# Forgetting attention and SwiGLU on one core: two query/key blocks turned by DMA, four wider gates, norm weights loaded in rows, an early table load and an order drawn from a list of seeds

## The chip, the cores and the metric

The kernel runs on one core of a Trainium2 chip. A core has TensorE (PE in the profile, with its weight loads shown apart as PEld), VectorE (DVE), ScalarE (ACT), GpSimd (POOL) and SyncE (SP), and 16 DMA engines that all of its queues share. The metric is the device time of one execution in microseconds (us); lower is better. The kernel before takes 385.1 us, the median of three runs (385.1, 385.17 and 381.8 us).

## The reference

```python
scores = scale * q @ k.T                            # 8 batches, 8 heads, 576 tokens, head size 64
cum = cumsum(log(clip(f, 1e-4, 1)))                 # a forget gate for each token and head
scores = where(causal, -1e9, scores + cum[i] - cum[j])
attn = softmax(scores);  o = attn @ v               # per batch and head
x = o, heads side by side                           # 4608 tokens x 512
xn = x / sqrt(mean(x * x) + 1e-6) * rms_g
g = xn @ w_gate;  val = xn @ w_val                  # 512 -> 1536
out = (g * sigmoid(g) * val) @ w_out                # 1536 -> 512
```

Inputs and output are f32.

## The kernel before

**The work.** A batch has 576 tokens: four blocks of 128 and one of 64 (the `LAST`). The decay needs no term in the scores: the `j` part, `exp(mid - cum[j])`, scales the rows of v (`scale_v`), an extra column of v carries the same factor so that the denominator comes out of the same matmul, and the `i` part cancels. So a block of attention is a score matmul (`score_block`, L444), an exp on ACT (L462), a causal mask on POOL for the diagonal block (L469), the values matmul (`values`, L488) and a division on DVE (L502, L504). `norm` then takes the squares on ACT (L520), the root on POOL (L524, L525), scales on ACT (L532) and turns the block, by PE and a DVE copy (L540, L548, L550) for batches 0 and 1 and by a DMA transpose on SP's queue (L554) for the others.

The feed-forward part works on nine groups of 512 tokens: groups 0 to 7 are the four whole blocks of batches 0 to 7, group 8 collects the eight 64-token rests. `gate` makes 512 columns of gate and of value: 4 matmuls of 128x512 each (one of the 12 slices of the inner width for all 512 tokens), or, in groups 0 and 1, 16 matmuls of 128x128 each (four slices for one block of 128 tokens, so that a gate waits for one block only). Then come tanh on ACT (L611) and two DVE operations (L613, L606). `project` multiplies with `w_out` (L624, three parts of 4 matmuls), ACT copies the result (L637) and SP stores it (L641, L650).

**How q and k are turned.** Scores need q and k with the head dimension in partitions. For batches 2 to 7 and for the 64-token rests of all batches, `turn` has SP issue one DMA transpose for q and one for k per block (L375). For the whole blocks of batches 0 and 1, `turn_pe` has PE transpose them and DVE (q) and ACT (k) copy them out of PSUM (L403): blocks 0 and 3 of batch 0 by themselves (L390), blocks 1 and 2 of batch 0, 0 and 1 of batch 1, and 2 and 3 of batch 1 in pairs (L396). A pair comes in by one load for q and one for k (`load_qk2`, L308: two rows of a head in one piece), a single block by `load_qk` (L296).

**The norm weights.** `rms_g` is loaded as 128 partitions x 4 by a DMA on ACT's queue behind the decay's exp (L268). Group 0's blocks are multiplied with it when they are copied (L548). For the others it is multiplied into `w_gate` and `w_val` by `weigh` (L338), after group 0 has used the plain weights.

**The decay.** One chain at the start: load f (SP), clip (DVE), ln (ACT, L255), cumulative sum (DVE, L261), exp (ACT, L266), five PE transposes (L275), copy (L279).

**What sets the order.** Nothing is written in order by hand. Each piece of work is a `Unit` with an engine, an assumed duration, a key, what it depends on, and the buffers it takes and gives back. `Plan.run` plays these through once on the host: whenever an engine is free it takes, of the units that are ready and whose buffers are free, the one with the smallest key. The order that results is the order of instructions on each engine, and each engine runs its own in order. DMA loads are played as an issue on the queue's engine (SP, ACT or POOL), a transfer that shares bandwidth with the other kind of queue (software for POOL, hardware for SP and ACT), and a landing time. Before the play, all keys are moved by a random amount of at most 0.02 (seed 12, L84 to L86).

Of the kernel before, what the change touches and what calls it, by code (L numbers as in the profile page):

```python
# [10 lines left out]
F32 = mybir.dt.float32  # L11
# [3 lines left out]
PSUM = bass.MemoryType.PSUM  # L15

# [16 lines left out]
class Plan:  # L33
# [8 lines left out]
    def add(self, eng, dur, key, emit, deps=(), take=(), give=(), lat=0.06):  # L42
# [32 lines left out]
    def run(self):  # L75
# [67 lines left out]
def fox_ffn_kernel(ctx, tc, q, k, v, f, moe_w_gate, moe_w_val, moe_w_out, moe_rms_g, out):  # L143
    nc = tc.nc
# [41 lines left out]
    rgT = sb.tile([128, NDC], F32, name="rgT")  # L186
    mhalf = sb.tile([128, NB], F32, name="mhalf")
# [13 lines left out]
    def pe(dur, key, emit, deps=(), take=(), give=()):  # L201
        return P.add("PE", dur, key, emit, deps, take, give, lat=0.22)

    def act(dur, key, emit, deps=(), take=(), give=()):
        return P.add("ACT", dur, key, emit, deps, take, give)

    def dve(dur, key, emit, deps=(), take=(), give=()):
        return P.add("DVE", dur, key, emit, deps, take, give)
# [3 lines left out]

    issues = {}

    def load(eng, issue, moves, key, emit, deps=(), take=(), give=(), late=1.6):
# [3 lines left out]
        u = P.add(eng, issue, key, emit, deps, list(take) + [lane], (), lat=2.0 if eng == "POOL" else 1.2)  # L219
# [5 lines left out]

    PLAIN = 1

# [29 lines left out]
    def emit_cum():  # L257
# [6 lines left out]

    d3 = dve(2.5, -19, emit_cum, [d2])
    d4 = act(0.9, -19, lambda: nc.scalar.activation(dec[:, 0:S], cum, ACT.Exp, scale=-1.0, bias=mid[:, 0:1]),  # L266
             [d3])
# [3 lines left out]
    h_dec = Hold("ff", 1 + EARLY)  # L271

    def emit_dect():
        for j in range(NB):
            nc.tensor.transpose(T_ff[h_dec.slot][:, j * 64:(j + 1) * 64], dec[:, j * 128:(j + 1) * 128],  # L275
                                ident_f[0:BH, 0:BH])

    d5 = pe(0.6, -19, emit_dect, [d4, iden_f], take=[h_dec])
# [11 lines left out]
    def load_qk(b, j, key):  # L290
        p0, n = rows(j)
        for src, nm in ((q, "q"), (k, "k")):
# [5 lines left out]
            qkload[b, nm, j] = load("POOL", 0.9 * n / 128, (8 * n, 0.0009), key, emit, take=[h])  # L298
            late.setdefault((b, j), []).append(issues[id(emit)])

    def load_qk2(b, j, key):

        t0 = j * 128
        for src, nm in ((q, "q"), (k, "k")):
# [5 lines left out]
            qkload[b, nm, j] = load("POOL", 0.9, (1024, 0.0016), key, emit, take=[h])  # L310

    def load_v(b, j, key):
# [7 lines left out]
        vload[b, j] = load(eng, dur, (64, 0.0155) if eng == "POOL" else (8 * n, 0.00117), key, emit, take=[h])  # L320
# [4 lines left out]
    def load_w(i, key):  # L325
        c0, c1 = i * 512, (i + 1) * 512
        for w, src, nm in ((wg, moe_w_gate, "g"), (wv, moe_w_val, "v")):
            def emit(w=w, src=src):
                nc.gpsimd.dma_start(out=w[:, :, c0:c1], in_=src[:, c0:c1].rearrange("(c p) f -> p c f", p=128))
            Lw[nm, i] = [load("POOL", 0.75, (512, 0.0061), key, emit, late=2.6)]  # L330
# [10 lines left out]
    def load_wo(key):  # L341
        for i in range(2):
# [4 lines left out]
            Lo.append(load("POOL", 0.85, (768, 0.0061), key, emit))  # L347
# [23 lines left out]
    def turn(b, j, key):  # L371
        p0, n = rows(j)
        for dst, nm in ((T_QT, "q"), (T_KT, "k")):
            def emit(dst=dst, nm=nm):
                nc.sync.dma_start_transpose(out=dst[hold_QT[b].slot][:, :, p0:p0 + n],  # L375
                                            in_=T_qk[hold_qk[b, nm, j].slot][0:n, :])
            turned[b, nm, j] = load("SP", 1.6, (4 * n, 0.00117), key, emit, [qkload[b, nm, j]],
                                    take=[hold_QT[b]], give=[hold_qk[b, nm, j]])
# [32 lines left out]
    def scale_v(b, j, key):  # L411
# [9 lines left out]
        add, dur, eng = (dve, 0.8 if b or j < EARLY else 1.2, nc.vector) if b < 2 else (pool, 1.3, nc.gpsimd)  # L421
# [89 lines left out]
    def norm(b, js, key):  # L511
# [4 lines left out]
        for i, j in enumerate(js):  # L516
# [4 lines left out]
            us.append(act(0.85, key, emit, [evac[b, j, 0], evac[b, j, 1]]))  # L521
# [5 lines left out]
        for i, j in enumerate(js):  # L527
# [6 lines left out]
            if g < 2:  # L534
# [9 lines left out]
                def cp(hf=hf, g=g, c=c):  # L544
                    tp = T_ff[hf.slot].bitcast(BF16)[:, 0:512].rearrange("p (c t) -> p c t", t=128)
                    to = T_of[g][hold_xT[g].slot][:, :, c:c + 128]
                    if g < PLAIN:
# [3 lines left out]
                pieces[b, j] = dve(0.69 if g < PLAIN else 0.42, key - 0.02, cp, [t, L_rg], take=[hold_xT[g]], give=[hf])  # L551
            else:
# [3 lines left out]
                pieces[b, j] = load("SP", 1.6, (4 * n, 0.00117), key, tr, [u], take=[hold_xT[g]], give=[hn])  # L556
# [12 lines left out]
    for b, qi in order:  # L569
        if b >= 2 or qi == LAST:  # L570
# [19 lines left out]
    def gate(g, key, deps, i, pairs):  # L590
# [22 lines left out]
        a = dve(0.72, key - 0.1, lambda: nc.vector.scalar_tensor_tensor(  # L613
            T_ga[ha.slot], in0=T_th[ht.slot], scalar=1.0, in1=T_ff[hg.slot], op0=ALU.add, op1=ALU.mult),
            [th], take=[ha], give=[ht, hg])
        return dve(0.72, key - 0.1, last, [a, uv], take=[hold_hT[g]], give=[ha, hv])

    def project(g, j, key):
        hf, ho = Hold("ff", 1), Hold("ores", 1)
        last = None  # L620
        for part in range(3):
# [5 lines left out]
            deps += hdone[g, j][part::3] if g < 2 else hdone[g, j][part * 4:part * 4 + 4]  # L627
# [25 lines left out]
    for g in range(G):  # L653
        if g < 2:
# [62 lines left out]
```

## Time and profile before

| | |
|---|---|
| runs | 385.1, 385.17, 381.8 us |
| the profiled execution, its own time | 382.67 us |
| its span | 380.9 us |
| PE, DVE, ACT, POOL busy | 94%, 57%, 62%, 53% |
| PE's clock as granted, mean | 0.997 |

A line of the profile names an engine, the line of the kernel, the operation and what it writes and reads. "Idle before" is the time in which the engine stood still just before such an instruction, and the name behind the arrow is what ended it. The times of several matmuls of a group overlap, because they are pipelined: sixteen 128x128 matmuls of 0.22 us each take 0.89 us together. "SPq" and "POOLq" are the queues that issue DMAs.

### The profile page before, as it was taken

Reading aid. Unit: us, or ns where it says so; the run is one execution under the profiler, and the core shown is the slowest. Engines: PE = TensorE matmul, PEld = TensorE weight load, DVE = VectorE, ACT = ScalarE, POOL = GpSimd, SP = SyncE. Lnnn points to the kernel's source line nnn. Section 1 sums busy time; section 2 is a strip of 40 time slices with the busy share of each in tenths; the row PEclk is TensorE's granted clock in tenths of the full one; section 3 lists DMA queues with packets and bytes.
Section 4 is the critical chain, followed back from the end, with each engine's and each line's share of the span. In section 5 each row is a group of like instructions: output and inputs, shape, how many; then the busy total and the mean of one; then the engine's idle time right before and its main releaser. Section 6 shows DMA issues by size and latency. Waiting matters only on the chain.

```text
span 380.9 us, 9695 instructions
## 1 busy us (share of the span) xinstructions
PE 358.7 (94%) x3941; PEld 212.4 (56%) x3941; DVE 218.0 (57%) x457; ACT 236.6 (62%) x377; POOL 200.6 (53%) x280
## 2 busy tenths in 40 slices
PE   1589799999999999999999999999999999999994
PEld 1479697788865455545555554455455544444441
DVE  4557998855555656544745565546655545454430
ACT  4486798778767676866676768665975433331321
POOL 8786579999799664964497369921411000000000
PEclk9999999999999999999999999999999999999998
DMA  9999999999999949995699979972120210100004
GB/s 147 180 202 220 214 98 174 142 190 170 164 187 179 163 95 147 142 167 80 98 183 147 106 108 165 199 65 56 36 58 28 57 34 29 55 28 29 28 29 110
DMA packets 129389, 44.84 MB, mean 118 GB/s; under 512 B 117824, under 2 KB 122432, under 8 KB 129344
## 3 DMA queue, kind: packets, MB, share of 16 engines
q0 software_dynamic: 76368, 23.34, 61.5%
q1 hardware_dynamic: 52368, 20.74, 29.2%
q8 instruction: 31, 0.51, 0.6%
q10 hardware_dynamic: 608, 0.13, 0.4%
q14 instruction: 14, 0.11, 0.1%
HBM read 37.90 MB, written 9.44 MB: 124 GB/s over the span
## 4 chain that ended last, share of the span: by engine, by line
PE 84%; DMA 5%; POOL 3%; ACT 3%; DVE 2%; issue 1%; SPq 0%; ACTq 0%; DVEq 0%; POOLq 0%
PE ff L599 45%; PE ff L624 24%; PE ff L488 7%; PE sc L444 6%; DMA qk<-in_k_dram 3%; DMA KT<-qk 2%; ACT PT L462 1%; POOL PT L469 1%; POOL qk L296 1%; ACT junk L520 1%; DVE x L504 1%; POOL v L319 1%; ACT th L611 0%; DVE xT L548 0%; DVE QT L403 0%
## 5 line engine op out<-in xcount | busy, mean ns | idle before, releaser
L613 DVE SCALAR_TENSOR_TENSOR ga<-th,ff 128x512 f32<-128x512 f32 x108 | 73.8, 685 | 85.4 <-ACT th L611 84.0
L624 PE MATMUL ff<-wo,hT 128*128 128x512 bf16 x432 | 108.9, 379 | 0.0
L611 ACT ACTIVATE th<-ff 128x512 f32<-128x512 f32 x108 | 64.3, 595 | 69.2 <-PE ff L599 59.8
L462 ACT ACTIVATE PT<-sc 128x1024 bf16<-128x1024 f32 x96 | 94.6, 1020 | 13.3 <-PE sc L444 13.1
L599 PE MATMUL ff<-xT,wg 128*128 128x128 bf16 (+1 forms) x672 | 97.5, 290 | 0.9 <-DVE xT L548 0.9
L599 PE MATMUL ff<-xT,wv 128*128 128x128 bf16 (+1 forms) x672 | 97.4, 288 | 0.0
L606 DVE SCALAR_TENSOR_TENSOR hT<-ga,ff 128x512 bf16<-128x512 f32 x108 | 72.7, 684 | 21.9 <-PE ff L599 19.6
L599 PEld LDWEIGHTS <-wg 128*128 128x128 bf16 x720 | 54.6, 99 | 37.6 <-issue 1.0
L599 PEld LDWEIGHTS <-wv 128*128 128x128 bf16 x720 | 53.3, 98 | 36.7
L624 PEld LDWEIGHTS <-hT 128*128 128x128 bf16 x432 | 40.0, 98 | 43.5
L469 POOL TENSOR_SCALAR_AFFINE_SELECT PT<-PT 128x1024 bf16<-128x1024 bf16 x32 | 35.4, 1106 | 48.1 <-ACT PT L462 48.0
L488 PEld LDWEIGHTS <-PT 128*128 128x128 bf16 x896 | 37.3, 98 | 14.0 <-POOL PT L469 2.6
L488 PE MATMUL ff<-Vs,PT 128*128 128x65 bf16 x896 | 42.7, 195 | 2.2 <-POOL PT L469 2.1
L419 POOL TENSOR_TENSOR Vs<-v,decT 128x512 bf16<-128x512 f32 (+1 forms) x30 | 31.6, 1052 | 13.3 <-DMA v<-in_v_dram 13.2
L637 ACT COPY ores<-ff 128x512 f32<-128x512 f32 (+1 forms) x36 | 20.8, 579 | 28.5 <-PE ff L624 27.7
L444 PE MATMUL sc<-QT,KT 64*128 64x128 bf16 (+1 forms) x960 | 34.4, 212 | 3.9 <-ACT PT L462 1.9
L504 DVE TENSOR_TENSOR x<-ff,rden 128x256 f32<-128x256 f32 (+1 forms) x80 | 33.8, 423 | 2.8
L444 PEld LDWEIGHTS <-KT 64*128 64x128 bf16 x960 | 24.4, 96 | 18.5 <-issue 13.9
L319 POOL DMA_DIRECT2D v<-in_v_dram x39 | 34.6, 890 | 0.0
L532 ACT ACTIVATE xn<-x,rs 128x512 bf16<-128x512 f32 (+1 forms) x40 | 27.5, 717 | 6.2 <-POOL rs L525 6.2
L296 POOL DMA_DIRECT2D qk<-in_q_dram x34 | 29.9, 881 | 0.8 <-POOLq L701 0.8
L520 ACT ACTIVATE junk<-x 128x512 bf16<-128x512 f32 (+1 forms) x40 | 25.1, 627 | 8.5 <-DVE x L504 8.4
(59 smaller groups left out, 206.4 us busy)
## 6 DMA issues: line engine op xcount, KB each, us to landing
out_dram<-ores SPq DMA_DIRECT2D x32, 256.0 KB, 3.7
v<-in_v_dram POOLq DMA_DIRECT2D x31, 256.0 KB, 5.4
qk<-in_q_dram POOLq DMA_DIRECT2D x26, 128.0 KB, 5.7
qk<-in_k_dram POOLq DMA_DIRECT2D x26, 128.0 KB, 6.1
wg<-in_moe_w_gate_dram POOLq DMA_DIRECT2D x3, 512.0 KB, 12.6
wv<-in_moe_w_val_dram POOLq DMA_DIRECT2D x3, 512.0 KB, 14.4
wo<-in_moe_w_out_dram POOLq DMA_DIRECT2D x2, 768.0 KB, 11.8
v<-in_v_dram POOLq DMA_DIRECT2D x8, 128.0 KB, 6.7
```

The costliest lines, as they stand in the source:

```text
L296: nc.gpsimd.dma_start(out=T_qk[h.slot][0:n, :].rearrange("p (h d) -> p h d", d=D), in_=src[b, :, p0:p0 + n, :].rearrange("h p d -> p h d"))
L319: queue.dma_start(out=T_v32[h.slot][0:n, :, :], in_=v[b, :, p0:p0 + n, :].rearrange("h p d -> p h d"))
L444: nc.tensor.matmul(t[:, par, c:c + n], lhsT=kt[r, p, kj * 128:(kj + 1) * 128], rhs=qt[r, p, qi * 128:qi * 128 + n], start=True, stop=True)
L462: nc.scalar.activation(T_of_p[hp.slot][:, 0:2 * half].rearrange("p (a c) -> p a c", a=2)[:, :, 0:cols], T_sc[h.slot][:, :, 0:cols], ACT.Ex ...
L469: nc.gpsimd.affine_select(out=d, in_=d, pattern=[[0, 8], [1, n]], compare_op=ALU.is_ge, fill=0.0, base=0, channel_multiplier=-1)
L488: nc.tensor.matmul(po[:, p, :], lhsT=T_of_p[h.slot][:, c:c + 128], rhs=vs[:, kj, 2 * p + par, :], start=(kj == 0), stop=(kj == qi))
L504: nc.vector.tensor_tensor(d, po[:, :, 0:D], bcast(r, D), ALU.mult)
L599: nc.tensor.matmul(T_ff[h.slot][:, c:c + n], lhsT=w[:, dc, fc * 128:(fc + 1) * 128], rhs=xT[:, dc, t0:t0 + n], start=(dc == 0), stop=(dc = ...
L606: nc.vector.scalar_tensor_tensor(hT, in0=three[0], scalar=0.5, in1=three[1], op0=ALU.mult, op1=ALU.mult)
L611: th = act(0.6, key - 0.1, lambda: nc.scalar.activation(T_th[ht.slot], T_ff[hg.slot], ACT.Tanh, scale=0.5), [ug], take=[ht])
L613: a = dve(0.72, key - 0.1, lambda: nc.vector.scalar_tensor_tensor(T_ga[ha.slot], in0=T_th[ht.slot], scalar=1.0, in1=T_ff[hg.slot], op0=ALU ...
L624: nc.tensor.matmul(T_ff[hf.slot], lhsT=T_hT[hold_hT[g].slot][:, fc, j * 128:(j + 1) * 128], rhs=wo[:, fc, :], start=(fc == 0), stop=(fc == ...
```

## The change

Six things are changed.

1. **Batch 1's blocks 2 and 3** (`DT1 = 1`) are loaded by four `load_qk` instead of two `load_qk2`, and turned by `turn` (four DMA transposes on SP's queue) instead of `turn_pe`.
2. **Group 1's last third** (`WIDE1 = 1`): its slices 8 to 11 are made by four gates of 512 tokens, each 4 matmuls of 128x512, instead of four gates of one block. These gates wait for all four blocks of batch 1.
3. **The norm weights** are loaded as 4 rows of 128 (`rg4`) by SP, turned by one PE transpose more beside the decay's five, and copied to `rgT` by DVE. The decay's transposes now wait for this load too.
4. **The exp table**: an exp of one element is issued on ACT behind the ln, while DVE makes the cumulative sum.
5. **The planner's durations** are set anew: engines start later, ACT's and DVE's units are shorter with longer latencies, most loads move faster and land sooner, the landing of q's and k's DMA transposes is set later, issues on SP shorter.
6. **The order**: the random move of all keys goes; in its place 45 seeds are applied one after the other, each of which moves a few of the units of low key (0.2%, 1% or 5% of them, by up to 0.03, 0.15, 0.6 or 2.0).

`XPE = 2` and `g == 0` in place of `PLAIN` say the same as before.

```diff
+XPE, DT1, WIDE1 = 2, 1, 1
+SEEDS = (474109, 55084, 500929, 233942, 854567, 648692, 410543, 286341, 870744, 460429, 912210, 178241, 119171,
...
-        draw = random.Random(12)
-        for u in self.units:
-            u.key += draw.uniform(-0.02, 0.02)
+        for seed in SEEDS:
+            draw = random.Random(seed)
+            share, amp = draw.choice((0.002, 0.01, 0.05)), draw.choice((0.03, 0.15, 0.6, 2.0))
+            end = draw.choice((-5, 0.0, 0.3, 0.6, 1.0))
+            for u in self.units:
+                if u.key < end and draw.random() < share:
+                    u.key += draw.uniform(-amp, amp)
...
     def act(dur, key, emit, deps=(), take=(), give=()):
-        return P.add("ACT", dur, key, emit, deps, take, give)
+        return P.add("ACT", dur - 0.08, key, emit, deps, take, give, lat=0.12)
...
+    for eng, t in (("SP", 0.8), ("POOL", 1.3), ("ACT", 2.0), ("DVE", 0.8)):
+        P.add(eng, t, -99, None)
...
-    def load(eng, issue, moves, key, emit, deps=(), take=(), give=(), late=1.6):
+    def load(eng, issue, moves, key, emit, deps=(), take=(), give=(), late=1.0):
...
-        u = P.add(eng, issue, key, emit, deps, list(take) + [lane], (), lat=2.0 if eng == "POOL" else 1.2)
+        u = P.add(eng, issue, key, emit, deps, list(take) + [lane], (), lat=1.35 if eng == "POOL" else 0.8)
...
+    def emit_first_exp():
+        nc.scalar.activation(junk[0:1, 0:1], fr[0:1, 0:1], ACT.Exp)
+
+    act(1.5, -18.9, emit_first_exp, [d2])
...
-    L_rg = load("ACT", 0.6, (512, 0.001), -18, lambda: nc.scalar.dma_start(
-        out=rgT, in_=moe_rms_g.rearrange("(c p) -> p c", p=128)), [d4])
+    L_rg = load("SP", 0.6, (4, 0.01), -15.9, lambda: nc.sync.dma_start(
+        out=rg4, in_=moe_rms_g.rearrange("(c p) -> c p", p=128)))
...
+        nc.tensor.transpose(T_ff[h_dec.slot][:, NB * 64:NB * 64 + NDC], rg4, ident_f[0:NDC, 0:NDC])
+
+    d5 = pe(0.7, -19, emit_dect, [d4, iden_f, L_rg], take=[h_dec])
+    c_rg = dve(0.1, -18.5, lambda: nc.vector.tensor_copy(rgT, T_ff[h_dec.slot][:, NB * 64:NB * 64 + NDC]), [d5],
+               give=[h_dec])
...
     for j in (0, 2):
+        if DT1 * 2 > 3 - j:
+            for i in (j, j + 1):
+                load_qk(1, i, -9.5 + i * 0.1)
+                load_v(1, i, -9.5 + i * 0.1)
+            continue
...
-        if b >= 2 or qi == LAST:
+        if b >= 2 or qi == LAST or (b == 1 and qi >= 4 - 2 * DT1):
             turn(b, qi, qkey(b, qi) - 0.25)
...
+        deps = [pieces[g, j] for j in range(4)] if g < B else [pieces[b, LAST] for b in range(B)]
+        for i in range(3):
+
+            if g == 0 or g == 1 and i < 3 - WIDE1:
                 for j in range(4):
+                    hdone[g, j, i] = [gate(g, g + (i * 4 + j) / 16, [deps[j]], i,
+                                           [(i * 4 + c, j * 128, 128, c * 128) for c in range(4)])]
+            else:
+                us = [gate(g, g + fc / 16, deps, i, [(fc, 0, GT, 0)]) for fc in range(i * 4, i * 4 + 4)]
+                for j in range(4):
+                    hdone[g, j, i] = us
```

More of the change, by code (lines that the diff above doesn't have):

```diff
@@ L376, in emit @@
                                             in_=T_qk[hold_qk[b, nm, j].slot][0:n, :])
[L377 to L378 removed]
+            turned[b, nm, j] = load("SP", 1.3, (16 * n, 0.00029), key, emit, [qkload[b, nm, j]],
+                                    take=[hold_QT[b]], give=[hold_qk[b, nm, j]], late=1.8)
     def turn_pe(b, j, two, key):
@@ L550, in cp @@
                         nc.vector.tensor_copy(to, tp)
-                pieces[b, j] = dve(0.69 if g < PLAIN else 0.42, key - 0.02, cp, [t, L_rg], take=[hold_xT[g]], give=[hf])
+                pieces[b, j] = dve(0.69 if g == 0 else 0.42, key - 0.02, cp, [t, c_rg], take=[hold_xT[g]], give=[hf])
             else:
```

56 lines of the change are left out of this document (24 added, 32 removed).

## The prediction, made before the changed kernel was run

> **What bounds the kernel now.** I read first the busy times and the DMA slices of the page, then the busy time by stage, then PE's waits of the first 80 us.
>
> ```profile
> span 380.9 us, 9695 instructions
> PE 358.7 (94%) x3941; PEld 212.4 (56%) x3941; DVE 218.0 (57%) x457; ACT 236.6 (62%) x377; POOL 200.6 (53%) x280
> ...
> DMA  9999999999999949995699979972120210100004
> ```
>
> PE is busy 94% of the span. The last row is the DMA engines' busy share in 40 slices of 9.5 us, in tenths: full from the start. By stage (length, then busy time of each engine, granted clock, DMA share, GB/s):
>
> ```profile
> 5.54:28.50 22.96, 15.20 (x208) 11.91 (x209) 11.83 (x29) 14.77 (x20) 18.82 (x25) 1.00 1.35 191
> 28.50:76.00 47.50, 43.56 (x888) 38.60 (x886) 42.60 (x97) 37.12 (x59) 37.34 (x50) 1.00 1.44 170
> 76.00:365.50 289.50, 289.50 (x2805) 157.29 (x2803) 159.38 (x311) 180.63 (x294) 140.09 (x197) 1.00 0.83 106
> ...
> 376.10:380.90 4.80, 0.00 (x0) 0.00 (x0) 0.38 (x1) 0.37 (x1) 0.00 (x0) 0.80 0.45 109
> ```
>
> The first column behind the length is PE. From 76 us on it does not stop until the last projections; behind 376 us come the last copy and store (4.80 us), which the change leaves alone. So there are two places to gain: PE's work itself, and its idle time before 76 us. That is 5.54 us until the first block of q has landed (the first row of the waits below), 22.96 - 15.20 = 7.76 us until 28.5 us, and 47.50 - 43.56 = 3.94 us until 76 us: 11.70 us behind the first landing. A microsecond of PE idle saved there is a microsecond of the end, as long as PE stays full behind it. Who ended these waits (total, times, longest):
>
> ```profile
> PE ff L390 <- DMA qk<-in_q_dram: 5.5, 1, 5.5
> PE ff L396 <- DMA qk<-in_k_dram: 2.4, 1, 2.4
> PE ff L488 <- POOL PT L469: 2.1, 2, 1.3
> PE sc L444 <- ACT PT L462: 1.9, 3, 1.3
> PE ff L275 <- ACT hT L266: 1.6, 1, 1.6
> PE sc L444 <- ACT KT L403: 1.0, 2, 0.7
> PE ff L599 <- DVE xT L548: 0.9, 1, 0.9
> PE sc L444 <- DMA KT<-qk: 0.8, 1, 0.8
> ```
>
> No wait is long; most are places where PE's fixed order put an instruction too early.
>
> **The change part by part.** Rows of the timeline, of the transposes on SP, of the DMA landings (KB each, median us to landing) and of the hardware queue between 49 and 77 us:
>
> ```profile
> 43.12 1.08 PE L396 MATMUL ff<-ident,qk 128*64 128x128 bf16 x32
> 45.02 1.32 ACT L403 COPY KT<-ff 128x1024 bf16<-128x1024 bf16 x1
> L375 SPq DMA_TRANSPOSE QT<-qk x32: 1177/1233/2078, 50.4 to 251.5; - x32
> qk<-in_k_dram POOLq DMA_DIRECT2D x26, 128.0 KB, 6.1
> qk<-in_k_dram POOLq DMA_DIRECT2D x3, 256.0 KB, 7.6
> KT<-qk SPq DMA_TRANSPOSE x32, 4.8
> q1 hardware_dynamic: 4416, 1.05, 34.7%
> wo<-in_moe_w_out_dram POOLq DMA_DIRECT2D x2, 768.0 KB, 11.8
> 35.02 1.65 POOL L344 DMA_DIRECT2D wo<-in_moe_w_out_dram  x2
> 65.72 1.04 PE L624 MATMUL ff<-wo,hT 128*128 128x512 bf16 x4
> ```
>
> *Batch 1's blocks 2 and 3.* The pair's 32 transposes stand at 43.12 us in a stretch where PE has work on both sides; the 1.08 us hold some 0.2 us of the last one's drain, beside which the next group starts, so I count **-0.9 us**. DVE and ACT lose one copy each (ACT's took 1.32 us), both off PE's path, though ACT's copy stands before exps that PE's values wait for (part of the 2.1 us behind the mask). Added are two issues on POOL (four loads for two, 0.9 us each: nothing waits for them but POOL's own masks, and those are the 2.1 us) and four transposes on SP, 1.23 us of issue each, landing 4.8 us later in the median. SP's queue is empty there: its first transpose is at 50.4 us. The DMA engines are not: in 49 to 77 us, twelve transposes on the hardware queue took 34.7% of 28 us, 0.8 us each, so four cost at most 3.2 us of a full resource. What hides them: what would be pushed back is `wo`, which is issued at 35.0 us, lands some 12 us later and is first read at 65.7 us. The price without cover: by PE, k is turned about 2.4 us after it has landed (1.08 + 1.32); by DMA the last of four comes 4 x 1.23 + 4.8 = 9.7 us after. If the scores of blocks 2 and 3 are not put later in the order, PE waits up to 7.3 us. I take 0 for it, nearest to the row of waits in which a late transpose cost PE 0.8 us in all of the start, and keep 0 to +7.3.
>
> By the Trainium skill, DMA: Bandwidth & Descriptors, Specifications, pieces under 512 B fall short of the line rate, which speaks against this part: the single loads read 256 B pieces where the pairs read 512 B. The rows lean the same way: 6.1 us to land a single block of k, 7.6 us a pair with twice the bytes; two singles one behind the other would be 4.6 us later than the pair, within the bound just given, and no more than that where they overlap.
>
> *Group 1's wide gates.* The chain gives 0.89 us to 16 matmuls of 128 columns and 0.86 us to 4 of 512:
>
> ```profile
> 86.79 0.89 PE ff L599 x16
> 254.55 0.86 PE ff L599 x4
> ```
>
> Four gates with two sides each: 8 x 0.03 = **-0.24 us**. They now wait for the last block of batch 1, but these are the last third of the group, and PE has whole gates, scores and projections to put before them: 0.
>
> *Norm weights and exp table.*
>
> ```profile
> 7.61 1.28 ACT L266 ACT_TABLE_LOAD   x1
> 9.82 0.76 PE L275 MATMUL ff<-ident_f,hT 64*128 64x64 f32 x5 [1.57 <-ACT hT L266]
> 3.88 2.01 POOL L319 DMA_DIRECT2D v<-in_v_dram  x2
> 6.75 0.91 POOL L308 DMA_DIRECT2D qk<-in_k_dram  x1
> 14.38 1.06 PE L396 MATMUL ff<-ident,qk 128*64 128x128 bf16 x16 [2.40 <-DMA qk<-in_k_dram]
> 20.66 1.17 PE L488 MATMUL ff<-Vs,PT 128*128 128x65 bf16 x16
> ```
>
> The table load of 1.28 us goes beside DVE's cumulative sum, so the decay's exp, the five transposes and the first exp of scores come up to 1.28 us earlier, and most of the 1.57 us wait goes. But PE then stands before the same k load, which lands at 14.3 us: alone, 2.40 us become some 3.7 us. I count **0**; the bound is -1.3 us if that load lands earlier too. The weights in rows add one transpose (0.76 / 5 = 0.15 us) and a small copy in the same hole, and a wait of the decay's transposes on a 2 KB load issued early on SP; 0, at most +0.3 us. That takes 512 pieces of 4 B off the DMA engines, which is not on PE's path.
>
> *The new durations and the searched order.* This is the part that the trace cannot price directly. It can touch the 11.70 us of idle and nothing else that is large, so its floor is -11.7. What is plainly order: the two v loads issued before the q and k of blocks 1 and 2 (3.88 to 5.89 us on POOL) hold the k load back by 2.01 us of issue and their transfer; what is made of that v is first multiplied at 20.7 us. Turned round, the 2.40 us wait shrinks by about 2. Whether the new durations fit the chip better the trace cannot say. I take **-2** of the 7.76 us before 28.5 us, where DMA supply limits whatever order does, and half of the 3.94 us behind it, **-2**. An order tuned to a model can also cost: PE, which has no idle at all behind 76 us, can only lose there. Ends: -11.7 and +5 (twice what the mask and the transposes, 2.1 + 0.8, cost now, less the 0.9).
>
> **The sum**: -0.9 - 0.24 - 2 - 2 = -5.1 us; span 375.8 us. Around the profiled span lie 382.67 - 380.9 = 1.8 us: 377.6 us. The profiled execution is 2.4 us below the median of the runs shown, two of which stand at 385; against those the same sum gives 380.0 us. I forecast the middle, **378.8 us**. About 1%, 3.9 us, is what a measurement of this kernel tells from no change.
>
> **The rivals.**
>
> *The order is worth nothing on the chip* (0.19). The waits are of many kinds and small, and removing one shows the next, as at the k load. Left are -0.9 and -0.24: 381.5 us from the profiled execution, 384.0 from the median. For it: DMA at 9 tenths in the first 13 slices, which no order makes faster.
>
> *The blocks turned by DMA come too late: slower* (0.17). Place: the scores of batch 1's blocks 2 and 3 at about 45 to 60 us. The chain shows what a transpose can take there:
>
> ```profile
> 59.71 9.29 DMA KT<-qk
> ```
>
> This one took 9.29 us and PE waited the 0.8 us of the last row of waits, because other work stood before it. It decides when PE reaches these scores before the last landing. The price is 7.3 us of waiting. If the rest holds, 7.3 - 5.1 = +2.2; if the order saves nothing, 7.3 - 1.1 = +6.2; with one landing as slow as this, 9.29 - 4.8 = 4.5 us more: +2 to +11. The 6.2 us, which I think likeliest of these, give 389 us from the profiled execution and 391 us from the median. Against it: group 0's gates are there to fill PE, as they did in the stage from 28.5 us, busy for 43.56 of 47.50 us.
>
> *The start closes up as a whole: more* (0.13). PE's matmuls run at half speed early and at full speed later:
>
> ```profile
> 18.73 0.61 PE L444 MATMUL sc<-QT,KT 64*128 64x128 bf16 x8 [1.27 <-ACT PT L462]
> 21.64 1.89 PE L599 MATMUL ff<-xT,wg 128*128 128x128 bf16 x16
> 24.46 1.06 PE L599 MATMUL ff<-xT,wv 128*128 128x128 bf16 x16
> ```
>
> The granted clock is 1.00 in both. The change of speed comes after a stretch that begins at 18.73 us and has no hole above 0.4 us. If the order closes the holes some 5 us sooner, 5 us of work run twice as fast (-2.5) on top of two thirds of the 7.76 us (-5.2) and the other terms (-3.1): -10.8, with a band of -8 to -11, 371.7 to 377 us. By the Trainium skill, TensorE: Matmul & The Clock Gate, part 1, the clock is at half rate until a window of about 3.4 us has been busy; the trace agrees (from 18.73 us to a point between 21.64 and 24.46 us). By that rule the gain is there only if holes go, not merely if the first matmul starts earlier.
>
> **How the numbers follow.** The forecast has 0.51, with a band of 376 to 381 us. Faster by over 1% (below 381.2 us): nearly all of it, all of the closed start, little of the worthless order: 0.64. Within 1%: most of the worthless order and the near end of the slower case: 0.23. Slower: 0.13. The range takes the forecast, the worthless order, most of the closed start and the near end of the slower case: 372.5 to 387.5 us.
>
> **What would show it.** The stage 76 to 365 us must keep PE without idle; the idle of 5.54 to 28.5 us should fall from 7.76 to about 6, that of 28.5 to 76 us from 3.94 to about 2. L396 should have 64 matmuls, not 96, and L599 96 fewer (128 to 32). The k load of blocks 1 and 2 should be issued ahead of the v loads and land before 14 us. A wait of L444 on KT or QT of over 2 us shows the slower case. Wrong I would be above all if the new order leaves holes behind 76 us, where there are none now.

## The result and the profile after

The changed kernel takes **385.98 us** in the median, the kernel before 383.87 us on the same chip. The ratio is 1.0074, with a 95% interval of 1.0053 to 1.0095: **0.7% slower**, 2.8 us by the ratio and 2.1 us by the medians, where I had forecast 378.8 us and 1.3% faster. The time is inside the range, and the change of time is inside the 1% that I had called no change, but its sign is wrong, and the interval excludes no change. The ratios leave out the few executions that ran slow as a whole, and since the first profile of the changed kernel fell on such a one, the rows below are of a second run of the same kernel, whose profiled execution took 388.06 us. That is 2 us above its median, and the profile before is of an execution 1.2 us below its own (382.67 us), so the two profiles lie 5.4 us apart, twice what the change costs.

The top of its page, and the slices of the granted clock and of the DMA engines:

```profile
span 386.3 us, 9401 instructions
PE 357.4 (92%) x3764; PEld 209.2 (54%) x3814; DVE 219.0 (57%) x457; ACT 236.7 (61%) x377; POOL 202.5 (52%) x282
...
PEclk9999998999999999999999999999999999999999
DMA  9999999999989998998899789992020210101004
```

By stage (length, busy time of PE, PEld, DVE, ACT and POOL, granted clock, DMA share, GB/s):

```profile
5.54:28.50 22.96, 16.33 (x218) 12.94 (x219) 11.26 (x30) 16.47 (x25) 20.01 (x27) 1.00 1.35 201
28.50:76.00 47.50, 40.81 (x678) 32.91 (x680) 40.04 (x86) 26.80 (x42) 33.42 (x41) 0.96 1.68 166
76.00:130.00 54.00, 50.55 (x813) 36.66 (x820) 32.27 (x72) 44.93 (x74) 47.54 (x70) 1.00 1.37 161
```

The third stage of the kernel before, for comparison (its first two stand in the prediction):

```profile
76.00:130.00 54.00, 54.00 (x804) 38.51 (x802) 31.45 (x68) 41.39 (x68) 49.48 (x70) 1.00 1.70 178
```

PE's idle time went from 7.76 to 22.96 - 16.33 = 6.63 us in the first stage, from 3.94 to 47.50 - 40.81 = 6.69 us in the second, and from nothing to 54.00 - 50.55 = 3.45 us in the third. The start is better by 1.1 us, of the 2 hoped for; the two stages behind it are worse by 2.8 and 3.4. Where the holes are, from PE's timeline (start, duration, in brackets the idle time before it and what ended it):

```profile
10.61 1.07 PE L421 MATMUL ff<-ident,qk 128*64 128x128 bf16 x16 [0.47 <-DMA qk<-in_k_dram]
59.97 0.28 PE L513 MATMUL ff<-Vs,PT 128*128 128x65 bf16 x4 [3.83 <-DVE ga L638]
80.31 0.29 PE L469 MATMUL sc<-QT,KT 64*128 64x64 bf16 x7 [1.04 <-issue]
117.88 0.82 PE L624 MATMUL ff<-xT,wg 128*128 128x512 bf16 x3 [1.38 <-DMA xT<-xn]
```

The first row is the k load of blocks 1 and 2: waited for 0.47 us, no longer 2.40. The second is new and the longest. It is a load of v that came late, as POOL and DVE show:

```profile
50.59 0.92 POOL L339 DMA_DIRECT2D v<-in_v_dram  x1 [5.62 <-DVE hT L631]
51.73 0.89 POOL L339 DMA_DIRECT2D v<-in_v_dram  x1 [0.22 <-issue]
...
58.15 0.69 DVE L444 TENSOR_TENSOR Vs<-v,decT 128x512 bf16<-128x512 f32 x1 [2.87 <-DMA v<-in_v_dram]
58.76 1.15 DVE L445 CAST Vs<-decT 128x8 bf16<-128x8 f32 x1
```

POOL stood 5.62 us before it issued the load, and what released it was an instruction of DVE; DVE could multiply the first v of the two then issued 58.15 - 50.59 = 7.6 us later, and PE, whose next instruction was the product with it, began 0.06 us after DVE's copy behind it had ended (58.76 + 1.15), 3.83 us late. The last row of the PE timeline is the new wait of group 2's first wide gate for its turned x.

A hole costs more than its length. The clock in the stretches behind the 3.83 us:

```profile
58.00:61.00 3.00, 1.03 (x10) 0.56 (x10) 2.85 (x5) 0.00 (x0) 3.00 (x4) 1.00 2.22 152
61.00:64.00 3.00, 1.90 (x14) 0.77 (x15) 2.93 (x9) 0.72 (x2) 3.00 (x5) 0.55 2.11 158
64.00:67.00 3.00, 3.00 (x42) 1.86 (x39) 2.63 (x8) 2.15 (x3) 2.23 (x3) 0.88 1.67 191
```

The granted clock falls to 0.55 and 0.88; on 1.90 and 3.00 us of work that is 0.45 x 1.90 + 0.12 x 3.00 = 1.2 us. The balance of the two profiled executions, by stages: -1.1 + 2.8 + 3.4 of idle, +1.2 of clock, -1.14 of PE work saved by the prediction's own terms: +5.2 us, and the spans differ by 386.3 - 380.9 = 5.4 us. It is an estimate, since the rows of the changed kernel have 3764 matmuls beside 3814 weight loads: 50 matmuls left no record. Most of these lie behind 130 us, where the rows leave 1.95 us empty and name no wait of PE; I take that for work.

### The profile page after: what moved, and what is told of

Read it like the earlier page. It is cut to its first block, busy times and chain, and to the rows that moved or that the text cites. A ratio compares the mean times of both kernels' runs of the same rounds, so it can differ in the third digit from the quotient of the medians.

```text
span 390.6 us, 9401 instructions
## 1 busy us (share of the span) xinstructions
PE 361.4 (93%) x3764; PEld 211.4 (54%) x3814; DVE 219.3 (56%) x457; ACT 236.8 (61%) x377; POOL 202.6 (52%) x282
## 4 chain that ended last, share of the span: by engine, by line
PE 76%; DMA 9%; DVE 6%; POOL 4%; issue 3%; ACT 1%; ACTq 0%; POOLq 0%; DVEq 0%
PE ff L624 43%; PE ff L649 21%; PE ff L513 6%; PE sc L469 6%; DMA v<-in_v_dram 4%; DMA wg<-in_moe_w_gate_dram 3%; DMA xT<-xn 2%; DVE ga L638 1%; POOL v L339 1%; POOL qk L316 1%; DVE hT L631 1%; DVE Vs L445 1%; DVE Vs L444 1%; DVE x L529 1%; POOL Vs L444 1%
## 5 line engine op out<-in xcount | busy, mean ns | idle before, releaser
L649 PE MATMUL ff<-wo,hT 128*128 128x512 bf16 x408 | 106.4, 383 | 1.2 <-DVE x L529 0.3
L624 PEld LDWEIGHTS <-wg 128*128 128x128 bf16 x672 | 51.8, 99 | 41.7 <-DMA xT<-xn 4.3
L624 PEld LDWEIGHTS <-wv 128*128 128x128 bf16 x672 | 51.5, 99 | 37.5 <-issue 1.1
L649 PEld LDWEIGHTS <-hT 128*128 128x128 bf16 x432 | 41.0, 99 | 46.8 <-issue 2.6
L513 PEld LDWEIGHTS <-PT 128*128 128x128 bf16 x896 | 38.7, 99 | 20.2 <-POOL PT L494 4.1
L513 PE MATMUL ff<-Vs,PT 128*128 128x65 bf16 x896 | 43.7, 197 | 5.7 <-POOL PT L494 3.5
L469 PE MATMUL sc<-QT,KT 64*128 64x128 bf16 (+1 forms) x960 | 35.9, 219 | 3.1 <-issue 1.5
L469 PEld LDWEIGHTS <-KT 64*128 64x128 bf16 x960 | 25.8, 99 | 17.2 <-issue 12.6
L527 DVE RECIPROCAL rden<-ff 128x4 f32<-128x4 f32 (+1 forms) x80 | 14.2, 177 | 34.7 <-PE ff L513 34.5
L316 POOL DMA_DIRECT2D qk<-in_q_dram x36 | 31.7, 882 | 2.8 <-DMA wo<-in_moe_w_out_dram 2.2
```

The source lines that it names most:

```text
L316: nc.gpsimd.dma_start(out=T_qk[h.slot][0:n, :].rearrange("p (h d) -> p h d", d=D), in_=src[b, :, p0:p0 + n, :].rearrange("h p d -> p h d"))
L469: nc.tensor.matmul(t[:, par, c:c + n], lhsT=kt[r, p, kj * 128:(kj + 1) * 128], rhs=qt[r, p, qi * 128:qi * 128 + n], start=True, stop=True)
L513: nc.tensor.matmul(po[:, p, :], lhsT=T_of_p[h.slot][:, c:c + 128], rhs=vs[:, kj, 2 * p + par, :], start=(kj == 0), stop=(kj == qi))
L624: nc.tensor.matmul(T_ff[h.slot][:, c:c + n], lhsT=w[:, dc, fc * 128:(fc + 1) * 128], rhs=xT[:, dc, t0:t0 + n], start=(dc == 0), stop=(dc = ...
L649: nc.tensor.matmul(T_ff[hf.slot], lhsT=T_hT[hold_hT[g].slot][:, fc, j * 128:(j + 1) * 128], rhs=wo[:, fc, :], start=(fc == 0), stop=(fc == ...
```

## The experiments

The change mixes operations (parts 1 to 4), the planner's durations (part 5) and the moves of keys that stand for the searched order (part 6). The theories: **A**, the new durations make the planner expect things earlier than the chip delivers them; **B**, the blocks turned by DMA cost; **C**, the searched order costs; **D**, seed 12 of the kernel before was a lucky draw. All times are medians; the kernel before took 383.0 to 384.4 us beside them, and the ratio is to it. Kernels are compared with each other by their ratios. "Kept" means that operations common to two kernels keep the same moves of keys.

**The changed kernel once more.**

> The changed kernel once more, for a second profile. In the first one PE waited 3.8 us at 119 us for the turned blocks of batch 2 (xT), 2.2 us at 59 us for a scaled v, and ran at half clock behind both. Theory A (the new durations let a DMA transpose land too early, so group 2's first gate stands too early in the order): the wait for xT is there again, 2 us or more, and the time is 385 to 387 us. Theory B (the two blocks turned by DMA crowd the DMA engines between 35 and 60 us): the wait at 59 us is there again and that for xT comes and goes. If both are gone, the first profile was of a disturbed execution and says little.

Measured: 386.06 us, ratio 1.0063 (1.0031 to 1.0095). The loss repeats.

**Part 6 undone.** The 45 seeds replaced by the old jitter of seed 12:

```
-        for seed in SEEDS:
...
+        draw = random.Random(12)
+        for u in self.units:
+            u.key += draw.uniform(-0.02, 0.02)
```

> The changed kernel with the 45 seeds taken out and the old move of all keys (seed 12, up to 0.02) put back: parts 1 to 5 without part 6. Theory A: the durations are at fault, so this is no faster than the changed kernel, 385 to 389 us, with a wait for xT. Theory C (the searched order itself is what costs): 380 to 384 us and no wait behind 80 us.

Measured: 395.11 us, 1.0275 (1.0206 to 1.0345), above both ranges expected. Against the old jitter the 45 seeds are worth 2%, some 8 us, on top of parts 1 to 5, and C falls: the changed kernel would be far slower without them. The question turns to parts 1 to 5.

**Parts 1 to 4 without 5 and 6**, first with new draws, then with kept moves; then part 1 left out, then part 2 left out (the flags `DT1` and `WIDE1`):

```
-XPE, DT1, WIDE1 = 2, 1, 1
+XPE, DT1, WIDE1 = 2, 0, 1
```

> The kernel before with parts 1 to 4 alone (blocks 2 and 3 of batch 1 by DMA, wide gates, weights in rows, early table load), old durations and old move of the keys. By the sum of the prediction -0.9 - 0.24: about 1 us faster than before, with PE full behind 80 us. Theory B: 2 us or more slower than before, with waits of PE for KT, QT or v between 40 and 70 us.

> Parts 1 to 4 on the kernel before, as in the run of parts 1 to 4, but now every unit that both kernels have keeps the very move of its key that it had before (units that are new get none). Theory D: most of the 4.3 us that parts 1 to 4 cost came from drawing anew, so this is 382 to 385 us. Theory B (the parts themselves cost, the blocks turned by DMA above all): 386 to 389 us again.

> The kernel before with parts 2 to 4 (wide gates, weights in rows, early table load), old durations, each shared unit with its old move of the key: the run of parts 1 to 4 with kept moves, less part 1. Theory B1 (the blocks turned by DMA are what costs): 383 to 385 us, and PE does not wait for batch 2's turned x near 118 to 126 us. Theory B2 (the wide gates are what costs, because gates that wait for one block no longer fill PE): 387 to 390 us, with that wait.

> Parts 1, 3 and 4 (blocks turned by DMA, weights in rows, early table load) without the wide gates, old durations and kept moves. B1: 387 to 390 us, with the wait for batch 2's turned x near 118 to 126 us. B2: 383 to 385 us, without it.

Measured: all four parts 388.19 us, 1.0111 (1.0059 to 1.0164), and with kept moves 389.85 us, 1.0134 (1.0054 to 1.0213); without part 1 385.07 us, 1.0025 (0.9984 to 1.0065); part 1 without the wide gates 389.57 us, 1.0132 (1.006 to 1.0203). In this order of the work part 1 goes with +1.1 to +1.3%, and the wide gates with nothing. Where it shows, in the kernel with parts 1 to 4:

```profile
118.91 1.89 PE L618 MATMUL ff<-xT,wg 128*128 128x512 bf16 x4 [5.47 <-DMA KT<-qk]
```

Not at the scores of blocks 2 and 3, where I had looked, but 60 us later, at the first gate of group 2: batch 2's chain of loads, scores and turned x runs late.

**Part 5 alone**, on the kernel before, with seed 12 and with seed 13, and seed 13 without it:

```
+    for eng, t in (("SP", 0.8), ("POOL", 1.3), ("ACT", 2.0), ("DVE", 0.8)):
+        P.add(eng, t, -99, None)
...
-        u = P.add(eng, issue, key, emit, deps, list(take) + [lane], (), lat=2.0 if eng == "POOL" else 1.2)
+        u = P.add(eng, issue, key, emit, deps, list(take) + [lane], (), lat=1.35 if eng == "POOL" else 0.8)
...
-        vload[b, j] = load(eng, dur, (64, 0.0155) if eng == "POOL" else (8 * n, 0.00117), key, emit, take=[h])
+        vload[b, j] = load(eng, dur, (64, 0.0130) if eng == "POOL" else (8 * n, 0.00117), key, emit, take=[h])
...
-        draw = random.Random(12)
+        draw = random.Random(13)
```

> The kernel before with the new durations (part 5) alone, old move of the keys. Theory A: slower than before by 2 us or more, with a wait of PE for xT near 110 to 130 us. Theories B and C: within 1 us of before, PE full behind 80 us.

> The kernel before with another draw for the move of the keys (seed 13 for 12), nothing else. Theory D (seed 12 is a lucky draw, and any change of the plan draws again; the new durations are innocent): 391 to 395 us, like the kernel with the new durations alone (394.0). Theory A (the new durations are at fault): 384 to 388 us, one draw from another costs less than 4 us.

> The kernel before with the new durations (part 5) and seed 13: the pair to the run before it, in which only the durations differ. Theory A: 5 us or more slower than that run, 390 to 396 us. Theory D: within 3 us of it.

Measured: the durations alone 394.04 us, 1.0266 (1.0215 to 1.0317). Seed 13 alone 388.25 us, 1.0113 (1.005 to 1.0176). Seed 13 with the new durations 391.24 us, 1.0209 (1.0162 to 1.0256). Without touching one operation, the kernel with the new durations is slower than its partner by 2.7% with seed 12 and by 1.0% with seed 13, some 10 and 4 us. D holds too: another jitter of 0.02 on the keys is worth 1.1%, some 4 us, by itself.

The pairs are not clean, though. The first lines of the edit put four units without work at the head of the list of units, and the moves are drawn along that list, so with the same seed each unit gets the move that was drawn for another. Each pair therefore compares two draws as well as two sets of durations, and the second difference is no larger than what a draw alone is worth, and below the 5 us that had been set as the mark of A. What speaks for A is the three orders with a plain jitter and the new durations together, at 1.0209, 1.0266 and 1.0275 (the last with parts 1 to 4 as well): the six such orders with the old durations that ran lie between 1 and 1.0134. Against A's account of the place: it had expected a wait for the turned x near 110 to 130 us, and from 100 to 140 us PE waits nowhere in the kernel with seed 12 and 0.4 us in the one with seed 13; the holes of the first are at 61 and 83 us.

**The 45 seeds on the old durations** (here four units of no length stand at the head of the list, so that each move stays on its unit), and the late load of v put back (its key exchanged with that of another v load of batch 1; `pin` marks the block's number):

```
+        p = {u.pin: u for u in self.units if hasattr(u, 'pin')}
+        p[0].key, p[3].key = p[3].key, p[0].key
         now = 0.0
```

> The changed kernel with the old durations: parts 1 to 4 and the 45 seeds, whose moves fall on the same units by the same amounts. Theory A (the new durations leave too little room, so the chip runs behind the plan): 2 us or more faster than the changed kernel, 380 to 384 us. If the seeds only suit the durations they were searched with: 387 us or more.

> The changed kernel with one exchange of keys: the load of v for batch 1, block 0, which the seeds had put behind every other load of batch 1 (it is issued at 50.6 us, lands at 57 us, and PE waits 2.2 to 3.8 us for what is made of it), takes the key of block 3's load and the other way round. If that one seed costs what the profile shows, the wait of 2.2 to 3.8 us and most of the half-clock stretch behind it (some 1.7 us) go: 380 to 383 us. If something else is late next (mask, v of block 3, the turned x of batch 2), 384 to 387 us.

Measured: 388.94 us, 1.0124 (1.0055 to 1.0193). By the mark set before, this speaks against A for this order (380 to 384 us had been its range) and for seeds that suit only the durations they are used with. With the v load put back 388.92 us, 1.01 (1.0006 to 1.0194), above both ranges expected: the hole of 3.83 us is gone, and nothing is gained, since the rest of the order slides and other holes of about 1 us open. To close one hole is not to repair an order.

**Orders searched anew.** A search of the same kind as that of the change (a list of seeds, each kept if the plan ends earlier by its own durations), on the old durations: for the kernel before, for part 1 with 3 and 4, for parts 2 to 4, and for parts 3 and 4 (kept moves in the last three). Each edit puts the loop of the change, with its own seeds, behind the old jitter:

```
+        for seed in (414002, 61981, 566950, 968298, 223021, ...):
+            draw = random.Random(seed)
...
+                    u.key += draw.uniform(-amp, amp)
```

> The kernel before with its own durations and its own seed, and behind them 22 further seeds that move some keys, found in the way the change found its 45. Nothing else of the change is in it. If searching an order is worth something by itself (the 45 seeds took 395.1 to 386.1 on the changed durations): 379 to 382, ratio 0.985 to 0.995. If the seeds of the change only won back what the new durations had lost, and the order of before is as good as a search makes it: 383 to 385, no effect. If a new draw is a lottery of which seed 12 was a good one (seed 13 gave 388.2): 386 to 389.

> The kernel with parts 1, 3 and 4 (blocks 2 and 3 turned by DMA, weights in rows, early exp table), narrow gates and old durations, which took 389.6, with 18 seeds searched for it. If part 1 costs in any order (its DMAs and its buffers delay batch 2): 387 to 390, and 4 or more above the searched kernels that leave it out. If its +1.3% was only that nobody had searched an order for it: 380 to 384, beside the other searched kernels.

> The kernel with parts 2, 3 and 4 and old durations, blocks 2 and 3 of batch 1 turned on PE as before (385.1 without a search), with 12 seeds searched for it. If a searched order is worth 1% where the durations are the old ones: 380 to 383, and this beats both kernels. If not: 384 to 387.

> The kernel before with parts 3 and 4 alone (weights in rows, early exp table), old durations, and 18 seeds searched for it. If searching is worth 1%: 380 to 383. Against the kernel with parts 2, 3 and 4 searched, the same within 0.5% if the wide gates are worth the 0.24 us that I gave them; 2 or more us slower if they are worth more. If the search is worth nothing: 384 to 387.

Measured: the kernel before, searched, 392.11 us, 1.0186 (1.0095 to 1.0278); with part 1 385.17 us, 1.0043 (0.9997 to 1.0089); with part 2 386.65 us, 1.0075 (1.0045 to 1.0106); **parts 3 and 4 alone 379.26 us, 0.9886 (0.9833 to 0.994)**, faster than both kernels. So a search on the old durations can lose 1.9% and gain 1.1%. With searched orders part 1 stands 0.3% ahead of parts 2 to 4 and 1.6% behind parts 3 and 4, its own partner without it: no cost of its own can be read from that, nor excluded. The stages of the fast one:

```profile
5.54:28.50 22.96, 17.04 (x236) 14.12 (x237) 11.81 (x32) 16.90 (x24) 19.47 (x28) 1.00 1.38 205
28.50:76.00 47.50, 46.02 (x834) 38.38 (x832) 43.30 (x94) 33.37 (x52) 34.34 (x44) 1.00 1.54 191
76.00:130.00 54.00, 53.27 (x851) 39.36 (x848) 31.48 (x69) 44.84 (x74) 49.03 (x71) 1.00 1.58 151
```

Its idle time is 5.92 + 1.48 + 0.73 = 8.1 us against 11.7 us before, 3.6 us less; its span is 377.4 us, 3.5 us less. The clock is 1.00 in all three, and no wait of PE behind 28.5 us is above 0.7 us. (The first row's 5.92 is 22.96 - 17.04, and so on.)

**How much is the draw.** The fast kernel with other seeds, the changed kernel with other seeds, and the changed kernel without part 1, searched for itself; in the last two the searched seeds stand behind the old jitter:

```
-        for seed in (414002, 61981, 566950, 968298, ...):
+        for seed in (306524, 641029, 991813, 556760, ...):
...
-        for seed in SEEDS:
+        draw = random.Random(12)
+        for u in self.units:
+            u.key += draw.uniform(-0.02, 0.02)
+        for seed in (581194, 914070, 827950, ...):
...
-XPE, DT1, WIDE1 = 2, 1, 1
+XPE, DT1, WIDE1 = 2, 0, 1
```

> Parts 3 and 4 with the old durations again, which took 379.3 with 18 searched seeds, now with 27 other seeds from a second search. If a searched order on the old durations is worth 1% when batch 1's blocks stay on PE: 378 to 382. If 379.3 was one lucky draw among orders that the chip scatters over some 10 us: 384 to 392.

> The changed kernel, all parts, with 30 seeds of another search in place of its 45. If its result is that of its parts: 385 to 388, with a wait for the turned x of batch 2 at the first wide gate again. If it is that of its draw: outside of this, between 378 and 394, with PE's holes at other places.

> The changed kernel without part 1 (blocks 2 and 3 of batch 1 turned on PE in a pair, as before), with the new durations and 18 seeds searched for it, since the 45 were searched with part 1 in place. If part 1 is what costs: 378 to 381. If the new durations mislead the order: 386 to 394, as with the durations alone. If neither and only the draw counts: anything from 379 to 392, with holes of over 2 us on PE where it is slow.

Measured: parts 3 and 4 with the second search 383.49 us, 0.9971 (0.9938 to 1.0004), 0.9% behind the first; the changed kernel with other seeds 394.57 us, 1.0245 (1.0179 to 1.0311), 1.7% behind its own 45; without part 1 389.03 us, 1.013 (1.0087 to 1.0173). So 386 is the result of one order, not of the parts, and taking part 1 out does not repair it.

What happened in the changed kernel with other seeds, by its chain of waits (start, duration, what):

```profile
66.98 1.11 POOL PT L497
68.10 1.70 POOL qk L319 x2
...
70.83 11.06 DMA qk<-in_q_dram
...
81.91 6.48 DMA QT<-qk
...
88.52 0.41 PE sc L472 x8
```

and in PE's timeline:

```profile
68.15 0.48 PE L516 MATMUL ff<-Vs,PT 128*128 128x65 bf16 x10 [2.54 <-POOL PT L497]
88.52 0.62 PE L472 MATMUL sc<-QT,KT 64*128 64x128 bf16 x16 [2.16 <-DMA QT<-qk]
```

A load of q takes 11.06 us from its issue, the transpose of it 6.48 us more, and PE stands before the scores. Twenty microseconds earlier it was a mask, which POOL took up behind loads, that left PE idle for 2.54 us. The places are others than in the kernel with the 45 seeds; the kind is the same.

All kernels by their durations:

| durations | ratio to the kernel before |
|---|---|
| old, 12 kernels | 0.9886, 0.9971, 1 (before), 1.0025, 1.0043, 1.0075, 1.0111, 1.0113, 1.0124, 1.0132, 1.0134, 1.0186 |
| new, 7 kernels | 1.0074 (the change), 1.01, 1.013, 1.0209, 1.0245, 1.0266, 1.0275 |

The median of the first row is 1.0093, of the second 1.0209. The change is the best of its row, and all of that row are slower than the kernel before.

The plans say where the two rows part. `Plan.run` needs no chip: run on the host for each of these kernels, it gives the time at which the plan ends. It is 382.4 us for the kernel before and 375.2 us for the changed one, so the plan promised 7.2 us that the chip did not give. The measured median lies 0.4 to 13.0 us above the end of the plan in the 12 kernels with the old durations (median 4.4) and 10.8 to 21.6 us in the 7 with the new ones (median 12.5). Nor does the end of the plan rank orders of one kernel: the two searches of parts 3 and 4 both end at 378.8 us and are 0.9% apart on the chip; the changed kernel with other seeds ends 2.2 us earlier than with its own and is 1.7% slower; the kernel before, searched, ends 3.3 us earlier and is 1.9% slower.

## Why the prediction was wrong

**The step that failed is the one on the new durations and the searched order.** I wrote that whether the new durations fit the chip better "the trace cannot say", and took -2 and -2 for both edits together. The trace could say it. By the diff, a load of v on POOL counts 0.9 of issue, then 2.0, then 64 x 0.0155, then 1.6: 5.5 us to landing before; with the new constants 0.9 + 1.35 + 64 x 0.0130 + 1.0 = 4.1 us, to which the planner adds what two transfers take from each other and their wait in the queue (in the plans run on the host, the median of POOL's v loads from issue to landing is 5.6 us before and 4.3 us in the changed kernel). A transpose of 128 rows of x goes from 1.6 + 1.2 + 0.6 + 1.6 = 5.0 us to 1.3 + 0.8 + 0.6 + 1.0 = 3.7 us. Beside that stand the landings of the kernel before (KB each, median us):

```profile
v<-in_v_dram POOLq DMA_DIRECT2D x31, 256.0 KB, 5.4
qk<-in_q_dram POOLq DMA_DIRECT2D x26, 128.0 KB, 5.7
qk<-in_k_dram POOLq DMA_DIRECT2D x26, 128.0 KB, 6.1
...
xT<-xn SPq DMA_TRANSPOSE x24, 4.2
```

and of the changed kernel:

```profile
v<-in_v_dram POOLq DMA_DIRECT2D x31, 256.0 KB, 6.2
qk<-in_k_dram POOLq DMA_DIRECT2D x28, 128.0 KB, 6.2
qk<-in_q_dram POOLq DMA_DIRECT2D x28, 128.0 KB, 4.7
...
QT<-qk SPq DMA_TRANSPOSE x34, 5.3
KT<-qk SPq DMA_TRANSPOSE x34, 5.6
...
xT<-xn SPq DMA_TRANSPOSE x24, 4.7
```

The old constant of v is that of the kernel before to 0.1 us; the new one is 2.1 us short of what the changed kernel met. In the pages of all kernels v's median lies between 5.2 and 6.7 us, under the new durations between 5.2 and 6.3, so 4.1 is short in each of them. The constants of q and k went from 0.9 + 2.0 + 0.9 + 1.6 = 5.4 us, beside 5.7 and 6.1 measured, to 4.1, beside 4.7 and 6.2. Those of their transposes, though one of their terms was set later, went from 5.0 to 4.5 us in all, beside 5.3 and 5.6. Of these rows only x's transpose was counted too long before, by 0.8, and is now too short by 1.0. An order made with such numbers puts PE's instruction ahead of its data, and PE's queue is in order: it stands.

At the hole at 59.97 us the landing is only a part of that. By the plan of the changed kernel its v load is issued at 45.97 us and lands at 51.84; on the chip it was issued at 50.59 and landed at 58.12. Of the 6.3 us of delay 4.6 were there before the issue, where POOL stood behind its plan, and 1.7 came in the landing. So what runs ahead of the chip is the plan as a whole, of which the landings are the part that the profile's rows price directly.

Shown are the late landings, the plans that promise too much, and that all seven kernels with the new durations are slower than the kernel before. That the durations are the cause is argued from these taken together; no pair with the same moves of keys was run, and which constants cost, those of the landings or those of the engines, was not run by itself. That the time still fell inside the range is luck: another draw of the order gave 394.57 us, outside of it, with the same operations and durations.

Point by point:

- **Blocks turned by DMA, -0.9.** L421 has 64 matmuls, as I said, and the 1.1 us of PE work are gone. The cover "`wo`" was the wrong thing to look at: what came late is batch 2. In the plain order the part cost 1.1%, some 4 us (1.0025 against 1.0134), within the bound of +7.3, though not at the scores of blocks 2 and 3; in searched orders on the old durations no cost stands clear of the scatter (385.17 with it; 379.26, 383.49 and 386.65 without). How it delays batch 2 (the longer queue on POOL, that on SP, or the twelve buffers that its four tiles now share) was not taken apart.
- **Wide gates, -0.24.** Too small to show: with them and the plain order 1.0025 (0.9984 to 1.0065). I gave their wait for the last block nothing, and no row of that kernel speaks against it.
- **Weights in rows, exp table, 0.** Not run by themselves without a search; with the wide gates they gave the 1.0025 just named. The k load came ahead and landed before 14 us, as the condition for the -1.3 had it; the first stage gained 1.1 us in all.
- **The order, -4 in all.** Its size was in reach: parts 3 and 4 with one search took 3.6 us out of PE's idle time, and the span was 377.4 us, beside the 375.8 us of my sum for all parts. But I treated the order as a gain to be halved, where the runs show a scatter: the same operations and durations gave ratios of 1, 1.0113 and 1.0186 (kernel before), 0.9886 and 0.9971 (parts 3 and 4), 1.0074, 1.0245 and 1.0275 (all parts). The upper end of +5 for "an order tuned to a model" was the right mechanism with too small a size and a chance that I didn't give it: +4 to +10 us with the new durations, each with its draw, then some -8 by the 45 seeds.
- **"Wrong I would be above all if the new order leaves holes behind 76 us."** It does: 3.45 us up to 130 us, 1.38 of them at one gate; and 6.69 us stand ahead of it, between 28.5 and 76 us.
- **The rivals.** The one with the blocks that come too late had its sign, not its place; the worthless order (381.5 to 384.0 us) is the nearest in time, 2 us short, and for another reason. The closed start came to 1.1 us of 7.76.

By the Trainium skill, TensorE: Matmul & The Clock Gate, part 1, the clock goes back to half rate after an idle window of about 3.4 us. Here less was enough, in three kernels: in the kernel with the new durations alone a hole of 2.58 us was followed by 32 matmuls in 3.51 us at a granted clock of 0.58,

```profile
83.09 3.51 PE L601 MATMUL ff<-xT,wg 128*128 128x128 bf16 x32 [2.58 <-DVE hT L608]
```

```profile
79.00:83.09 4.09, 1.46 (x21) 0.77 (x20) 4.09 (x4) 2.95 (x4) 4.06 (x5) 0.99 1.22 211
83.09:87.00 3.91, 3.91 (x43) 3.91 (x43) 1.92 (x3) 0.96 (x2) 3.91 (x6) 0.58 0.84 157
```

and in the changed kernel without part 1 one of 3.32 us by 16 matmuls in 1.87 us, where 16 such take 1.05 us a little later:

```profile
80.37 1.87 PE L633 MATMUL ff<-xT,wv 128*128 128x128 bf16 x16 [3.32 <-DVE ga L647]
...
83.75 1.05 PE L633 MATMUL ff<-xT,wv 128*128 128x128 bf16 x16
```

and in parts 3 and 4 with the second search one of 2.07 us, behind which 16 took 1.90 us:

```profile
81.72 0.28 PE L523 MATMUL ff<-Vs,PT 128*128 128x65 bf16 x4 [2.07 <-DVE hT L643]
...
82.67 1.90 PE L636 MATMUL ff<-xT,wv 128*128 128x128 bf16 x16
```

The price in the first of these is (1 - 0.58) x 3.91 = 1.6 us on top of the 2.58. But the length alone does not decide it: with part 1 and without the wide gates a hole of 3.18 us, in which no weight load is recorded either, left the granted clock at 1.00 up to 100 us:

```profile
96.06 1.02 PE L654 MATMUL ff<-wo,hT 128*128 128x512 bf16 x3 [3.18 <-issue]
```

I had used this rule for the start alone and gave no hole in the middle a price beyond its length.

## What to carry to other kernels

Where a planner's costs are part of a change, put each constant of the diff beside the row of the profile that measures the same thing, before anything else: the seven plans here that counted v's landing 1 to 2 us too early all lost time on the chip. A statically ordered kernel scatters by 1 to 2% between orders that its plan holds for equal, so an effect of a part is shown only over several orders, and an order is to be chosen by its time on the chip, not by the end of its plan. The profile of the fastest order here is plain to see: no wait of PE above 0.7 us once the first blocks are in, and a granted clock of 1.00.

## What was not expected of the hardware

- Behind the four holes shown above, of 2.07 to 3.83 us in the middle of the kernel, PE ran at about half its clock for some 2 to 4 us (0.55 and 0.58 granted, or 16 matmuls in 1.9 us); behind the one of 3.18 us it did not, and the holes of 1.0 and 1.4 us of the changed kernel left it at 1.00 in the third stage. What decides between 2 and 3.3 us no run here shows.
- DVE's small copy of the decay took 0.18 us or ten times as long, in two places 1.3 us apart in the changed kernel, and the long one lies beside a load that POOL issues and a mask on POOL:

```profile
38.75 0.18 DVE L445 CAST Vs<-decT 128x8 bf16<-128x8 f32 x1
...
39.23 1.47 POOL L339 DMA_DIRECT2D v<-in_v_dram  x2
...
40.02 1.83 DVE L445 CAST Vs<-decT 128x8 bf16<-128x8 f32 x1
...
40.67 1.13 POOL L494 TENSOR_SCALAR_AFFINE_SELECT PT<-PT 128x1024 bf16<-128x1024 bf16 x1
```

It ends at 41.85 us, as the mask does at 41.80. The copy at 58.76 us that PE waited for is one of the long ones, with 1.15 us. Loads alone do not make them: the copies at 10.12, 12.44 and 13.45 us, each beside a load that POOL issues, took 0.19 us. By the Trainium skill, SBUF — State Buffer, section on the two separate sides, DVE and GpSimd take a shared pair of ports as an exclusive lock, and a load issued from POOL needs it for its descriptors. The long copies agree with it and the short ones beside loads do not, so that the lock is the cause no run here shows.
